# A second mixture whose matmul operands lie 32 bytes apart modulo 512 in SBUF instead of at equal remainders

## The chip, the core and the metric

The kernel runs on one core of a Trainium2 chip. The metric is the device time of one execution in microseconds (us), the median of several runs. The engines are called as the profile calls them: PE (TensorE matmuls), PEld (TensorE's weight loads, which overlap PE), DVE (VectorE), ACT (ScalarE), POOL (GpSimd) and SP (the queue that issues most DMAs).

## What is computed

Three layers follow each other, in fp32: a windowed attention over 4 batches, 8 heads, 576 positions, 64 dimensions; a first mixture, in which each of 2304 tokens goes to one of 8 experts; and a second one, dense, through which all 2304 tokens go. The change touches the last alone:

```python
def _moe_ref(x, ...):                       # first mixture, per expert e
    h = np.maximum(x[mask] @ w1[e], 0.0)    # 512 -> 1024
    out[mask] = gate_w[mask, None] * (h @ w2[e])

def _moe2_ref(x, w_in, w_out):              # second mixture
    h = x @ w_in                            # 2304x512 @ 512x2048
    g = h * np.cos(h)
    return (g @ w_out).astype(np.float32)   # 2304x2048 @ 2048x512
```

## The kernel before

**Three products for one.** Every large fp32 product is made of three matmuls on operands of type fp32r: each operand is split into a high part and a rest, and high x high, high x rest and rest x high are summed in PSUM. So `wi_a`, `yT`, `gg` and the others have a dimension of 2 (`a` or `b` in the code): part 0 and part 1.

**Roles.** In `nc.tensor.matmul(out, lhsT, rhs)` the second argument is loaded into the array as weights (128 columns of 4 bytes, 512 bytes in each partition), the third streams past it (the moving operand, 256 or 512 columns). The row of PEld for a matmul is the load of its weights; it runs while the matmul before it streams.

**Second mixture, up (`up2`, line 1325).** For a group of 4 times 128 tokens and a tile `f` of 128 hidden columns (16 of them) there are 12 matmuls: 4 pieces of the 512 inputs (`kk`) times 3 products. The weights are a slice of `wi_a` (f below 8) or `wi_b` (f from 8), the moving operand is `yT`, 512 columns:

```python
nc.tensor.matmul(ph, wi[:, a, fi, 128 * kk:128 * kk + 128], yT[:, b, kk], ...)
```

Behind it ACT and DVE form `r = ph * cos(ph)` and split it into `gg`.

**Second mixture, down (`down2`, line 1353).** Here `gg` is the weights and `wo_a` or `wo_b` the moving operand, 512 columns; again 12 matmuls for a tile `f` (4 token tiles times 3 products):

```python
nc.tensor.matmul(ACC[s][t], gg[:, a, cs], wo[:, b, fo], ...)
```

PE's order is 12 of up, 12 of down for the tile two steps before, 12 of up, and so on, over segments `segs` (line 1321). There are 5 groups of tokens; the last has 2 token tiles only, so that `yT` is 256 columns wide there, and its `gg` lies in the other `yT` tile (lines 1408 and 1409; the trace then calls it yT). Some `wi` and `wo` halves (the b ones) are converted from their 64-bit form while the mixture already runs (`conv`).

**First mixture (`up`, `down`).** The same three products, in blocks of 12, with a moving operand of 256 columns: weights `s1_*` and `s2_*` (trace: s), moving operands `xT*` and `hh`. Its last unit (`unit_parts`, line 1003) is turned round: weights `xT` and `hh2` (trace: hh), moving operand `s`, 512 columns.

**Where tiles lie.** Tiles are allocated in stacks from both ends of SBUF, so a tile's byte address in a partition follows from what was allocated before it. An unused tile (`gap0`, line 944, `gap3`, line 1310) shifts what comes behind it. All parts and slices of the tiles below are whole multiples of 512 bytes apart, so that one remainder modulo 512 holds for each tile. In the built program of the kernel before they are:

| place | weights (remainder) | moving operand (remainder) | weights minus moving |
|---|---|---|---|
| first mixture, up and down | s 320 | xT, hh 288 | +32 |
| first mixture, last unit | xT, hh2 288 | s 320 | -32 |
| second mixture, up | wi_a, wi_b 320 | yT 320 | 0 |
| second mixture, down | gg 320 (also in yT) | wo_a, wo_b 320 | 0 |

Of the kernel before, what the change touches and what calls it, by code (L numbers as in the profile page):

```python
# [8 lines left out]
F32 = mybir.dt.float32  # L9
# [20 lines left out]
def kernel(  # L30
# [42 lines left out]
    def pool(c, name, bufs, side="left"):  # L73
        return c.enter_context(tc.tile_pool(name=name, bufs=bufs, side=side, reuse_waits="tile"))
# [860 lines left out]
    wi_h = [wres.tile([128, 2, NA, KD * 128], F32R, name="wi_a")]  # L935
    wo_h = [wres.tile([128, 2, NA, DM], F32R, name="wo_a")]
    yt0 = pool(ctx, "yt0", 1)
    ytiles = [yt0.tile([128, 2, KD * 512], F32R, name="yT0")]
    W1, W2, HH, ACC = {}, {}, {}, {}
    NF = FF // 128  # L940
# [364 lines left out]

    with ExitStack() as c:
        wb = pool(c, "wb", 1, "right")
        wi_h.append(wb.tile([128, 2, NA, KD * 128], F32R, name="wi_b"))
        wo_h.append(wb.tile([128, 2, NA, DM], F32R, name="wo_b"))
        wb.tile([128, 32], F32, name="gap3")  # L1310
        hpi = wb.tile([128, 1], F32, name="hpi")
        fp = pool(c, "fp", 2, "right")
        yp = pool(c, "yp", 4, "right")
# [151 lines left out]
```

## Time and profile before

| | |
|---|---|
| median of 3 runs | 843.32 us (842.28 to 845.54) |
| the profiled execution, its own time | 844.73 us |
| its span, first to last instruction | 843.0 us |
| granted TensorE clock, mean | 0.989 of full speed |
| PE / DVE / ACT / POOL busy | 95% / 73% / 58% / 24% of the span |

Attention takes the first fifth of the span, the first mixture the time to 435 us, the second the rest. A row of the timeline merges instructions of one kind that follow each other: its time is from the first one's start to the last one's end. A matmul's own duration contains its latency, so that rows overlap; the time that a block costs is the distance between its start and the start of the next.

### The profile page before, as it was taken

How to read it: one execution, taken by the hardware profiler on the slowest of the kernel's cores; microseconds unless marked ns; L12 is line 12 of the kernel's file. 1: busy time of each engine (PE TensorE's matmuls, PEld its weight loads, DVE VectorE, ACT ScalarE, POOL GpSimd, SP SyncE). 2: the span in 40 equal slices, each digit the busy share in tenths (PEclk: the TensorE clock that was granted, in tenths of full speed). 3: DMA queues.
4: the chain of work that ended last, by engine and by line, in shares of the span. 5: the costliest groups of instructions: out<-in, count | busy, mean ns of one | idle time of the engine just before them, and what ended most of it. 6: DMA issues, size and time to landing. Idle time of an engine off the chain costs nothing. (4 is left out here: it accounts for less than half of the span.)

```text
span 843.0 us, 14736 instructions
## 1 busy us (share of the span) xinstructions
PE 801.4 (95%) x5269; PEld 705.8 (84%) x5269; DVE 614.7 (73%) x1463; ACT 492.1 (58%) x912; POOL 201.2 (24%) x259
## 2 busy tenths in 40 slices
PE   7899999979899999999999999999999999999996
PEld 5789888969799999999878778787788888888995
DVE  3866686668889999996749989896665555555562
ACT  6675677534557576664637676764554454444562
POOL 5655565510122132230001121112212001100100
PEclk9899999989999999999999999999999999999999
DMA  8555441044788888869433232501312001100000
GB/s 158 141 143 126 120 120 38 28 148 141 260 278 273 273 284 278 267 221 335 158 125 100 80 106 73 176 25 51 112 38 75 1 1 37 38 1 0 26 26 25
DMA packets 125134, 103.40 MB, mean 123 GB/s; under 512 B 61725, under 2 KB 105027, under 8 KB 125059
## 3 DMA queue, kind: packets, MB, share of 16 engines
q1 hardware_dynamic: 122099, 92.74, 36.3%
q0 software_dynamic: 2960, 9.70, 3.2%
q8 instruction: 42, 0.69, 0.3%
q14 instruction: 33, 0.27, 0.1%
HBM read 85.90 MB, written 16.52 MB: 121 GB/s over the span
## 5 line engine op out<-in xcount | busy, mean ns | idle before, releaser
L1079 PE MATMUL bk<-hh,s 128*128 128x256 f32 x864 | 117.7, 284 | 7.8 <-DVE y L1079 4.6
L1079 PEld LDWEIGHTS bk<-hh,s 128*128 128x128 f32 x864 | 107.8, 188 | 10.1 <-DVE y L1079 5.6
L1079 PE MATMUL bk<-xT,s 128*128 128x256 f32 x864 | 114.5, 282 | 1.7 <-DVE s L1079 1.1
L1079 POOL TENSOR_TENSOR lf<-lf,mag 128x512 f32<-128x512 f32 x32 | 46.9, 1467 | 282.1 <-DVE mag L1079 246.9
L1079 PEld LDWEIGHTS bk<-xT,s 128*128 128x128 f32 x864 | 107.4, 188 | 2.2 <-DVE s L1079 1.3
L1079 ACT CAST s<-r 128x1024 fp32r<-128x1024 f32 x72 | 75.2, 1050 | 54.4 <-DMA r<-in_moe_w_dram 40.4
L1079 PE MATMUL bk<-yT,wi_a 128*128 128x512 f32 (+1 forms) x480 | 104.4, 368 | 1.2 <-DVE yT L1079 0.8
L1079 PE MATMUL bk<-yT,wi_b 128*128 128x512 f32 (+1 forms) x480 | 105.0, 368 | 0.0
L1079 DVE TENSOR_TENSOR s<-r,s 128x1024 fp32r<-128x1024 f32 x72 | 94.3, 1313 | 13.6 <-ACT s L1079 13.2
L1079 ACT ACTIVATE r<-r 128x512 f32<-128x512 f32 (+1 forms) x80 | 47.2, 590 | 92.5 <-DVE r L1079 92.5
L1079 PEld LDWEIGHTS bk<-yT,wi_a 128*128 128x128 f32 x480 | 84.0, 188 | 17.3 <-DVE yT L1079 1.1
L1079 PEld LDWEIGHTS bk<-yT,wi_b 128*128 128x128 f32 x480 | 84.6, 188 | 15.7
L1079 DVE TENSOR_TENSOR r<-bk,r 128x512 f32<-128x512 f32 (+1 forms) x80 | 50.9, 636 | 62.1 <-ACT r L1079 61.4
L1079 PE MATMUL bk<-wo_b,gg 128*128 128x512 f32 x384 | 93.7, 391 | 2.5 <-DVE po L1079 1.1
L1079 PE MATMUL bk<-wo_a,gg 128*128 128x512 f32 x384 | 92.8, 390 | 0.6 <-DVE gg L1079 0.5
L1079 PEld LDWEIGHTS bk<-wo_b,gg 128*128 128x128 f32 x384 | 71.4, 188 | 19.7 <-ACT o L1079 1.5
L1079 PEld LDWEIGHTS bk<-wo_a,gg 128*128 128x128 f32 x384 | 71.8, 188 | 16.5 <-DVE gg L1079 1.5
L1079 DVE TENSOR_TENSOR gg<-r,gg 128x512 fp32r<-128x512 f32 x64 | 46.1, 720 | 34.3 <-ACT gg L1079 34.3
L494 PE MATMUL bk<-vt,pT 128*128 128x65 f32 x544 | 66.8, 276 | 0.1
L494 PEld LDWEIGHTS bk<-vt,pT 128*128 128x128 f32 x544 | 65.1, 195 | 1.2 <-issue 1.0
L1079 ACT CAST gg<-r 128x512 fp32r<-128x512 f32 x64 | 39.7, 620 | 41.1 <-DVE r L1079 40.2
L1079 DVE SCALAR_TENSOR_TENSOR r<-ki,bk 128x512 f32<-128x512 int32 (+1 forms) x80 | 50.4, 630 | 16.5 <-ACT ki L1079 15.9
(280 smaller groups left out, 1279.5 us busy)
## 6 DMA issues: line engine op xcount, KB each, us to landing
r<-in_moe_w_dram SPq DMA_DIRECT2D x72, 512.0 KB
y_dram<-y SPq DMA_DIRECT2D x19, 256.0 KB
rqk<-in_q_dram SPq DMA_DIRECT2D x32, 128.0 KB
rqk<-in_k_dram SPq DMA_DIRECT2D x32, 128.0 KB
vt<-in_v_dram SPq DMA_DIRECT2D x32, 128.0 KB
x_dram<-xt SPq DMA_DIRECT2D x16, 256.0 KB
f64x<-in_moe_w_in_dram SPq DMA_DIRECT2D x8, 512.0 KB
raw<-in_moe_w_dram SPq DMA_DIRECT2D x8, 512.0 KB
```

The lines of the kernel that those rows point to most:

```text
L494: self.last = op(*args, **kwargs)
L1079: r = op(*args, **kwargs)
```

## The change

Two unused tiles of 32 bytes are added, ahead of `yT0` and ahead of `wi_b`, and `gap3` shrinks from 128 to 64 bytes. No other line changes.

```diff
     yt0 = pool(ctx, "yt0", 1)
+    yt0.tile([128, 8], F32, name="gap1")
     ytiles = [yt0.tile([128, 2, KD * 512], F32R, name="yT0")]
...
         wb = pool(c, "wb", 1, "right")
+        wb.tile([128, 8], F32, name="gap2")
         wi_h.append(wb.tile([128, 2, NA, KD * 128], F32R, name="wi_b"))
         wo_h.append(wb.tile([128, 2, NA, DM], F32R, name="wo_b"))
-        wb.tile([128, 32], F32, name="gap3")
+        wb.tile([128, 16], F32, name="gap3")
         hpi = wb.tile([128, 1], F32, name="hpi")
```

In the built program `yT0`, `yT1`, `gg` and the work tiles of the second mixture (f64x, raw, mag, top, lf, ki, r, yg, gb, o, po) come to remainder 352, `wi_b` and `wo_b` to 384; `wi_a` and `wo_a` stay at 320, and nothing of the first mixture's operands moves:

| second mixture | weights | moving operand | weights minus moving | matmuls |
|---|---|---|---|---|
| up with wi_a | 320 | yT 352 | -32 | 384 of 512 columns, 96 of 256 |
| up with wi_b | 384 | yT 352 | +32 | 384 of 512 columns, 96 of 256 |
| down with wo_a | gg 352 | 320 | +32 | 432 of 512 columns |
| down with wo_b | gg 352 | 384 | -32 | 432 of 512 columns |

Each engine has the same instructions in the same order. One wait moves, on SP's queue, at the start of the second mixture, where the tiles of the second group of tokens are fetched (yg is a tile of tokens, gb its gates; names behind `waits` are the semaphores of engines and DMA queues). Before:

```order
L967 DMA yg<-y_dram 128x4x128 [waits DMAHW1_49,DMAHW2_49,DVE_49,DMAHW3_49,PE_49,Activation_49]
L968 DMA gb<-g_dram 128x128 [waits DMAHW4_49]
L967 DMA yg<-y_dram 128x4x128 [waits DMAHW5_49]
L968 DMA gb<-g_dram 128x128 [waits DVE_49,DMAHW6_49,PE_49,Activation_49]
L967 DMA yg<-y_dram 128x4x128 [waits DMAHW7_49]
```

And now:

```order
L968 DMA yg<-y_dram 128x4x128 [waits DMAHW1_49,DMAHW2_49,DVE_49,DMAHW3_49,PE_49,Activation_49]
L969 DMA gb<-g_dram 128x128 [waits DVE_49,DMAHW4_49,PE_49,Activation_49]
L968 DMA yg<-y_dram 128x4x128 [waits DMAHW5_49]
L969 DMA gb<-g_dram 128x128 [waits DMAHW6_49]
L968 DMA yg<-y_dram 128x4x128 [waits DMAHW7_49]
```

The wait for PE, DVE and ACT, which stood at the second gb, stands at the first, one yg and one gb earlier: the first gb tile, 32 bytes further on, now reaches into a tile of the first mixture that is released later.

## Rows read from the trace of the kernel before

**Rows 1.** Page, part 1: busy time, share of the span, instructions

```profile
PE 801.4 (95%) x5269; PEld 705.8 (84%) x5269; DVE 614.7 (73%) x1463; ACT 492.1 (58%) x912; POOL 201.2 (24%) x259
```

**Rows 2.** Windows: the second mixture in three stretches and as a whole

```profile
435.60:592.60 157.00, 153.10 (x662) 123.39 (x662) 133.79 (x220) 99.61 (x171) 28.59 (x21) 1.00 0.28 89
592.60:785.40 192.80, 192.76 (x851) 159.62 (x851) 110.47 (x162) 97.12 (x156) 20.88 (x17) 1.00 0.09 30
785.40:836.00 50.60, 50.60 (x313) 45.36 (x312) 27.81 (x69) 27.73 (x69) 4.96 (x5) 1.00 0.06 22
435.60:836.00 400.40, 396.45 (x1824) 328.38 (x1824) 272.07 (x449) 224.46 (x394) 54.42 (x43) 1.00 0.16 52
```

**Rows 3.** Chain that ended last, from 592 us: start, us, what

```profile
592.66 240.74 PE bk L1079 x1150
833.39 0.02 issue
833.42 0.70 DVE o L1079
834.12 0.27 issue
834.38 2.72 DMA out_dram<-o,tok_d
```

**Rows 4.** Waits of PE, 435 to 592 us: total us, times, longest

```profile
PE bk L1079 <- DVE po L1079: 1.1, 2, 0.9
PE bk L1079 <- ACT o L1079: 1.1, 1, 1.1
PE bk L1079 <- DVE yT L1079: 0.8, 1, 0.8
PE bk L1079 <- DVE gg L1079: 0.5, 1, 0.5
PE bk L1079 <- PEq L1281: 0.5, 1, 0.5
PE bk L1079 <- ACT gg L1079: 0.3, 1, 0.3
```

**Rows 5.** Timeline of PE, second mixture, 512 columns: start, us, what, count

```profile
603.22 2.88 PE L1079 MATMUL bk<-wo_b,gg 128*128 128x512 f32 x12
605.94 2.88 PE L1079 MATMUL bk<-yT,wi_b 128*128 128x512 f32 x12
```

**Rows 6.** Timeline of PE, second mixture's last group: 256 and 512 columns

```profile
793.82 7.36 PE L1079 MATMUL bk<-yT,wi_a 128*128 128x256 f32 x60
801.01 1.55 PE L1079 MATMUL bk<-wo_a,yT 128*128 128x512 f32 x6
802.40 1.60 PE L1079 MATMUL bk<-yT,wi_a 128*128 128x256 f32 x12
...
826.39 9.71 PE L1079 MATMUL bk<-wo_b,yT 128*128 128x512 f32 x42
```

**Rows 7.** Timeline of PE, first mixture, 256 columns

```profile
343.78 1.58 PE L1079 MATMUL bk<-xT,s 128*128 128x256 f32 x12
345.20 1.58 PE L1079 MATMUL bk<-hh,s 128*128 128x256 f32 x12
```

**Rows 8.** Timeline of PE, first mixture's last unit, 512 columns

```profile
425.37 1.56 PE L1079 MATMUL bk<-s,xT 128*128 128x512 f32 x6
426.77 1.55 PE L1079 MATMUL bk<-s,hh 128*128 128x512 f32 x6
```

**Rows 9.** Tile hh: durations min/median/max of the last unit's matmuls

```profile
L1079 PE MATMUL bk<-s,hh x24: 388/394/502, 426.8 to 433.4; 128*128 128x512 f32 x24
```

**Rows 10.** Timeline of PE, second mixture's start and a block behind a stall

```profile
435.68 11.16 PE L1079 MATMUL bk<-yT,wi_a 128*128 128x512 f32 x48 [0.46 <-PEq L1281]
446.68 5.60 PE L1079 MATMUL bk<-wo_a,gg 128*128 128x512 f32 x24
```

**Rows 11.** Tiles wi_a and wi_b on DVE: durations min/median/max

```profile
L1079 DVE TENSOR_TENSOR top<-top,wi_a x8: 676/680/1794, 244.4 to 309.4; 128x512 f32<-128x512 f32 x8
L1079 DVE TENSOR_TENSOR top<-top,wi_b x8: 676/678/693, 456.6 to 553.2; 128x512 f32<-128x512 f32 x8
```

**Rows 12.** Timeline of SP's queue and of DVE at the second group's fetch

```profile
440.32 0.40 SPq L967 DMA_DIRECT2D yg<-y_dram  x1
440.76 0.50 SPq L968 DMA_DIRECT2D gb<-g_dram  x1
441.31 0.42 SPq L967 DMA_DIRECT2D yg<-y_dram  x1
441.90 0.38 SPq L968 DMA_DIRECT2D gb<-g_dram  x1
...
452.14 1.78 DVE L1079 TENSOR_TENSOR yg<-yg,gb 128x512 f32<-128x512 f32 x1
```

## Prediction, made before the changed kernel ran

> **What bounds the kernel now.** I read the busy times first: PE is busy for 95% of the span, DVE for 73% [rows 1]. A busy PE may still be waiting, so I cut the second mixture into stretches [rows 2]. From 592.6 to 785.4 us PE is busy for 192.76 of 192.80 us, at the full granted clock; from 785.4 to 836 us for all of it. In the first stretch, 157 us long, it idles for about 4 us and DVE is busy for 133.79 us. The chain of waits agrees: its last long piece is 240.74 us of PE alone, 1150 matmuls, and behind it come only one eviction and one store [rows 3]. So in this half of the kernel the spacing of the matmuls is the time: 1824 matmuls in 400.4 us [rows 2].
>
> Then I read the spacing. At 512 columns 12 matmuls start 605.94 - 603.22 = 2.72 us apart, 226.7 ns each [rows 5]. At 256 columns 60 matmuls take 801.01 - 793.82 = 7.19 us, 119.8 ns each, and 120.0 without the first one, which is short [rows 6]. The difference, 106.7 ns for 256 columns, is one column per cycle of the 2.4 GHz level. What is left over is 13.3 ns per matmul, the same at both widths. Over 1824 matmuls that is 24.3 us, all that a better placing of the operands could bring if it removed the whole of it.
>
> **Does the placing matter at all?** The first mixture has weights and moving operand 32 bytes apart already, and there 12 matmuls of 256 columns take 345.20 - 343.78 = 1.42 us, 118.3 ns [rows 7], against 120.0 at equal remainders: 1.7 ns less. Its last unit has the distance the other way, at 512 columns. Six of its matmuls take 426.77 - 425.37 = 1.40 us, 233.3 ns [rows 8], and the six behind them, whose last lasts 394 ns by the median [rows 9], are (1.55 - 0.394) / 5 = 231.2 ns apart: together 232.3 ns, 5.7 ns more than at equal remainders. These two rows are the only ones on operands 32 bytes apart, and they point in opposite directions.
>
> The second of them needs care. At equal remainders too a block of 6 that stands behind 256-column matmuls takes 802.40 - 801.01 = 1.39 us, 231.7 ns [rows 6]. But there the excess dies out: the last 42, (9.71 - 0.39) / 41 = 227.3 ns on average [rows 6], are nearly at 226.7. The same behind a stall: the first 48 of the second mixture take 11.00 us, 229.2 ns each, and by the end of them the rate is the steady one [rows 10]. In the last unit the second six are no faster than the first to speak of. I read this as two modes: at equal remainders the stream settles after some ten matmuls into a regular spacing of 226.7 ns, and at 512 columns 32 bytes apart it stays at the rate of the unsettled ones, 232 to 233 ns.
>
> **The change, term by term.**
>
> 1. *512 columns, 1632 matmuls* (768 up, 864 down, by the diff's table). The price of +32 bytes at this width is in no row. The bounds: the first mixture's gain, -1.7 ns, from a row of another width but of this sign [rows 7], and the last unit's loss, +6.6 ns by its first six [rows 8], from a row of this width but, for half of the matmuls, of the other sign. I take +6.0, between the two blocks of six, for both signs, since the width is what the spacing hangs on and up and down alternate every 12 matmuls: a block that would settle has only 12 to do it in. 1632 x 6.0 = +9.8 us.
> 2. *What is already at that rate* does not get slower: 16 blocks of 6 behind 256 columns, 0.03 us each, and the matmuls behind the start and the stalls, about 0.12 us for the start [rows 10] and as an estimate half of that for each of eight stalls. About 0.9 us, so -0.9.
> 3. *256 columns, 192 matmuls*: -1.7 ns each as in the first mixture [rows 7], -0.3 us; at worst the few ns of term 1 with the other sign, under 1 us.
> 4. *Cover in the first stretch.* A slower PE gives DVE more time there. Of PE's waits those for gg and yT, 0.5 + 0.8 + 0.3 us, end with DVE's or ACT's work [rows 4] and shrink; those for an eviction (po, o), 2.2 us, come behind PE's own last matmul and stay. -0.8 us, between 0 and -1.6.
> 5. *DVE, ACT and DMA on the shifted tiles*: nothing. The same DVE operation takes 680 ns on work tiles at remainder 288 and 678 at 320 [rows 11].
> 6. *The moved wait on SP.* The first gb and the second yg behind it are issued when the second gb was, 441.90 instead of 440.76, so about 1.1 us later [rows 12]; DVE first reads them at 452.14. Those 10 us cover it; without the cover it would cost the 1.1 us once.
>
> Sum: 9.8 - 0.9 - 0.3 - 0.8 = +7.8 us. On the span of 843.0 us that makes 850.8, on the profiled execution's 844.73 us it makes 852.5, and on the median of the runs, 843.32 (1.4 below that execution), **851.1 us**, 0.9% slower.
>
> **The rivals.**
>
> *The sign decides.* Weights 32 bytes behind the moving operand gain as in the first mixture, 32 bytes ahead lose as in its last unit. By the diff's table the 512-column matmuls are then split evenly: 816 x 6.0 - 816 x 1.7 = 4.9 - 1.4 = +3.5, less about 0.8 for terms 2 and 4: 846.0 us. For it: both rows are then explained as they stand. Against it: the two blocks alternate, and a settled spacing hardly survives the change.
>
> *All gain as in the first mixture.* 1824 x 1.7 = 3.1 us less, 840.2 us. For it stands the one long and steady row [rows 7]; against it that it has the other width.
>
> *The left-over time goes.* If the 13.3 ns are a conflict of the weight load with the stream and 32 bytes resolve it at 512 columns, the kernel is faster. The point from which this decides is 2.6 ns per matmul (4.2 us over 1632); half of the 13.3 ns would bring 1632 x 6.7 = 10.9 us on a PE that has no cover over 243 us of it, and less in the first stretch, where DVE is busy for 85% [rows 2]: about 833 us. Against it: the first mixture, already 32 bytes apart, keeps 11.7 of its 13.3 ns [rows 7]. The Trainium skill, page "TensorE: Matmul & The Clock Gate", section "Back-to-back issue gap", gives N / 2.4 + 2.5 ns for an isolated matmul, 215.8 at 512 columns; this trace has 226.7, and if the change reached the page's figure it would bring some 17.8 us.
>
> *The placing does nothing.* The spacing does not hang on addresses, the 1.7 ns come from what else the first mixture does, and the last unit is slow because it never settles: 843.3 us. The trace speaks against it with two regular rates that differ where only address and surroundings do, 118.3 and 120.0 ns [rows 6, 7]. The Trainium skill says on the same page, in "Step-by-step: what each phase is for", that moving operand and weight load have a read port each, so that a load takes nothing from the running matmul; by that rule this rival is the right one, and the two rates do not fit it.
>
> **How the numbers follow.** A difference under 0.5%, 4.2 us, can hardly be told from none. The forecast, all 512-column matmuls unsettled, gets 0.48; its own range is 848 to 855, from term 1 at 4.5 to 6.6 ns with the other terms at their ends, up to 1 us for 256 columns and 1 us for SP. Sign decides: 0.20. No effect: 0.12. Gain as in the first mixture: 0.11. Left-over time goes: 0.09. Slower by over 0.5% (above 847.5): the 0.48 and 0.05 of the sign rival, 0.53. Faster (below 839.1): the 0.09 and 0.02 of the gain rival, 0.11. Within: 0.36. The range from 840.0 to 855.5 leaves out the last rival, a part of the gain rival and a worse loss at 256 columns, some 0.18.
>
> **What would show it.** Right: PE's timeline from 592 us on has blocks of 12 that start 2.78 to 2.80 us apart instead of 2.72, and PE's chain of 1150 matmuls is about 6 us longer; the stretch before 435 us is unchanged. The sign rival shows blocks of two lengths, wi_a and wo_b long, wi_b and wo_a short. The gain rivals show every block under 2.72 us. Wrong would also be a new wait of PE for yT near 474 us (the moved wait on SP), or blocks that still settle at 2.72.

## The result and the profile after

Four executions of the changed kernel took 851.92 to 855.1 us, median 852.37; four of the kernel before, run beside them, 842.28 to 845.54, median 843.87. The ratio is 1.0094, with a 95% interval from 1.007 to 1.0118: slower, by 8.5 us. A second comparison on one chip, with 10 executions against 31, gave medians of 851.59 and 846.61 us and a ratio of 1.0061 (1.0022 to 1.0100). So the loss is clear of no change, and its size is nearer to 5 us than the first comparison says; what is known of the difference comes below.

Page of the kernel after, part 1 (busy time, share of the span, instructions), beside [rows 1]:

```profile
span 850.5 us, 14736 instructions
PE 812.2 (96%) x5269; PEld 708.7 (83%) x5269; DVE 614.7 (72%) x1463; ACT 493.6 (58%) x912; POOL 200.2 (24%) x259
```

The same instructions, DVE as busy as before, PE busy for 10.8 us more. The timeline of PE of the kernel after, from the stretch in which PE waits for nothing, beside [rows 5]:

```profile
630.65 2.96 PE L1080 MATMUL bk<-yT,wi_a 128*128 128x512 f32 x12
633.45 2.96 PE L1080 MATMUL bk<-wo_a,gg 128*128 128x512 f32 x12
636.25 2.96 PE L1080 MATMUL bk<-yT,wi_a 128*128 128x512 f32 x12
639.05 2.96 PE L1080 MATMUL bk<-wo_a,gg 128*128 128x512 f32 x12
```

Every block of 12 now takes 2.80 us, 233.3 ns per matmul, where it took 2.72. In the first row the weights lie 32 bytes behind the moving operand (at the lower remainder: wi_a 320, yT 352), in the second 32 ahead (gg 352, wo_a 320): both cost the same. The windows of the second mixture, cut at the same matmuls as [rows 2] (the 1st, the 663rd, the first of the last group, the end), of the kernel after:

```profile
438.80:594.60 155.80, 155.27 (x662) 123.84 (x662) 133.94 (x220) 99.63 (x171) 28.64 (x21) 1.00 0.28 90
594.60:792.95 198.35, 198.35 (x851) 159.62 (x851) 110.58 (x161) 97.42 (x156) 20.83 (x17) 1.00 0.09 29
792.95:843.55 50.60, 50.60 (x313) 44.88 (x311) 27.93 (x69) 27.79 (x69) 5.01 (x5) 1.00 0.06 23
438.80:843.55 404.75, 404.22 (x1824) 328.35 (x1824) 272.45 (x449) 224.85 (x394) 54.47 (x43) 1.00 0.16 52
```

The second mixture is 4.35 us longer. The middle stretch is 5.55 us longer, 198.35 us against 192.80, the last one is as long as before, and the first, whose matmuls are slower too, is 1.2 us *shorter*: PE is busy there for 155.27 us instead of 153.10, and idle for 0.5 us instead of 3.9. What happened there stands in PE's waits, 438 to 595 us (total us, times, longest), of the kernel after, beside [rows 4]:

```profile
PE bk L1080 <- ACT xg L1080: 0.7, 1, 0.7
PE bk L1080 <- PEq L1282: 0.5, 1, 0.5
PE bk L1080 <- DVE yT L1080: 0.4, 1, 0.4
```

The first of these lies ahead of the second mixture. Gone are the waits for po, o and gg, 2.2 us for evictions among them; the one for yT is halved. The chain that ended last, beside [rows 3], shows where it does cost:

```profile
593.84 247.03 PE bk L1080 x1154
```

The piece of PE alone is 6.3 us longer, with four matmuls more in it, which are worth 0.9 us (an estimate, 4 x 0.233). Behind it come the same eviction and the same store.

The rest of this execution's difference lies ahead of the change: its second mixture starts at 438.80 us, 3.2 us later than before. Two windows of 10 us from the first mixture (PE busy, granted clock, DMA share, GB/s), kernel after first, kernel before second, and the first of the two from a control with all operands at the old remainders (`c1_moved_ident`, below) third:

```profile
250.00:260.00 10.00, 8.10 (x55) 0.85 0.92 280
400.00:410.00 10.00, 8.22 (x60) 0.86 0.58 205
```

```profile
250.00:260.00 10.00, 8.56 (x70) 1.00 0.96 299
400.00:410.00 10.00, 8.52 (x73) 1.00 0.43 141
```

```profile
250.00:260.00 10.00, 8.12 (x58) 0.88 0.91 288
```

In the kernel after the granted clock fell to its lower level, 1.2 GHz, for a while in each of the two, and 15 and 13 matmuls fewer stand there. At 0.118 us each [rows 7] that is 3.3 us, an estimate that agrees with the 3.2. In the first window no tile is in use that the change moves; in the second DVE fills yT0 and reads raw, which have moved. That the change is not needed for such a fall is shown by the control, and the changed kernel runs without one there in its second profile below. The executions of the second comparison agree: mean clocks from 0.970 to 0.989 and times from 841.34 to 854.22 us in 31 of the kernel before, clocks from 0.972 to 0.991 in 10 of the changed one.

### The profile page after: what moved, and what is told of

Its sections match the earlier page's. It is cut to its first block, busy times and chain, and to the rows that moved or that the text cites. A ratio compares the mean times of both kernels' runs of the same rounds, so it can differ in the third digit from the quotient of the medians.

```text
span 850.5 us, 14736 instructions
## 1 busy us (share of the span) xinstructions
PE 812.2 (96%) x5269; PEld 708.7 (83%) x5269; DVE 614.7 (72%) x1463; ACT 493.6 (58%) x912; POOL 200.2 (24%) x259
## 5 line engine op out<-in xcount | busy, mean ns | idle before, releaser
L1080 PE MATMUL bk<-hh,s 128*128 128x256 f32 x864 | 119.8, 287 | 7.4 <-DVE y L1080 3.6
L1080 PEld LDWEIGHTS bk<-hh,s 128*128 128x128 f32 x864 | 110.1, 192 | 9.6 <-DVE y L1080 4.4
L1080 PE MATMUL bk<-yT,wi_b 128*128 128x512 f32 (+1 forms) x480 | 107.4, 372 | 0.0
L1080 PE MATMUL bk<-yT,wi_a 128*128 128x512 f32 (+1 forms) x480 | 106.4, 372 | 0.9 <-PEq L1282 0.5
L1080 PE MATMUL bk<-wo_a,gg 128*128 128x512 f32 x384 | 94.7, 396 | 0.0
```

Of the source, the lines that this page charges most:

```text
L1080: r = op(*args, **kwargs)
```

## The experiments

The kernels below, the changed kernel itself and the two on the first mixture excepted, need more room in SBUF than is left. For them the identity tile, 512 bytes, moves from one pool to another, which keeps every remainder:

```diff
-    ident = const.tile([128, 128], F32, name="ident")
+    ident = rt.tile([128, 128], F32, name="ident")
```

Single executions are not compared by their time below, since what lies ahead of the second mixture scatters by over 10 us between them; the timelines are.

### Control: the identity tile moved, nothing else

> The identity tile (512 bytes) lies in another pool, so that 512 bytes are free for paddings later; all operands keep their remainders modulo 512. Every theory: no change, ratio within 0.5% of 1, blocks of 12 in the second mixture 2.72 us apart. If the changed kernel's 3.1 us ahead of the second mixture are chance dips of the clock, this kernel's runs have mean granted clocks that scatter like the changed kernel's (0.980 to 0.986); if the change causes them, this kernel stays at about 0.989.

Measured: ratio 0.9991 (0.9965 to 1.0017), blocks of 12 at 2.72 us. Its ten executions have mean clocks from 0.969 to 0.989, so dips of the clock come without the change. Its windows, cut as above:

```profile
437.20:592.70 155.50, 152.33 (x662) 123.61 (x662) 133.76 (x220) 99.80 (x171) 28.61 (x21) 1.00 0.28 90
592.70:785.50 192.80, 192.76 (x850) 159.59 (x851) 110.74 (x161) 96.92 (x156) 20.83 (x17) 1.00 0.10 30
```

The first stretch was 157.00 us in the kernel before and is 155.50 here with the same operands, so that 1.5 us there are scatter; the middle one is 192.80 again. In the first stretch PE is busy for 152.33 of 155.50 us, and DVE does the same 133.8 to 133.9 us of work in all three kernels.

### The changed kernel again

> The changed kernel once more. Placing theory: the second mixture, first up to last down, lasts 404 to 405 us against 400.0 before, blocks of 12 at 2.80 us, and what lies ahead of it starts it at 435.7 us plus 1.7 us for each chance dip of the clock, so that a run without more dips than before is 4 to 5 us slower (848) and not 8.5. Rival, that the change costs time ahead of the second mixture too: it starts at 438 us or later again, at mean clocks of 0.986 or less in every run, 852 us.

Measured: ratio 1.0061 (1.0022 to 1.0100). Its profiled execution had a mean clock of 0.991, started the second mixture at 433.8 us and took 847.58 us. Its windows:

```profile
433.80:590.00 156.20, 155.43 (x662) 123.78 (x662) 133.72 (x220) 99.72 (x171) 28.63 (x21) 1.00 0.28 89
590.00:788.40 198.40, 198.40 (x852) 159.68 (x852) 110.81 (x161) 97.61 (x156) 20.80 (x17) 1.00 0.09 29
```

So 198.4 us in the middle again, 405.15 for the whole, and no loss ahead of it. Against the kernel before (400.4) the change costs 4.4 and 4.75 us in two profiles, against the control (398.95) 5.8 and 6.2; that is the size of the second comparison's 5.0. Of the first comparison's 8.5 us, then, some 3 should lie ahead of the second mixture. In the one execution that was profiled they do, with the two falls of the clock; that it was so in the other three is likely by their mean clocks, 0.980 to 0.986, but not shown.

### Up alone 32 bytes apart

```diff
+    yt0.tile([128, 8], F32, name="gap1")
```

> Only yT moves (remainder 352, weights wi at 320); gg, wo and all else stay at equal remainders. Theory that each block settles by its own remainders: up blocks 2.80 us, down blocks back at 2.72 to 2.75 after some five matmuls, the second mixture about 2.5 us longer. Rival, that an unsettled block carries over into the next 12: up and down blocks both at 2.78 to 2.80, as long as the changed kernel's second mixture, 4.4 us longer.

In the last group gg lies in yT, so that down's weights are 32 bytes ahead there; the rows below lie ahead of it. Timeline of PE:

```profile
641.17 2.92 PE L1080 MATMUL bk<-wo_a,gg 128*128 128x512 f32 x12
643.93 2.97 PE L1080 MATMUL bk<-yT,wi_a 128*128 128x512 f32 x12
646.74 2.92 PE L1080 MATMUL bk<-wo_a,gg 128*128 128x512 f32 x12
649.49 2.73 PE L1080 MATMUL bk<-yT,wi_a 128*128 128x512 f32 x11
```

Up blocks take 2.81 us, down blocks 2.75 to 2.76. The means of a down block's twelve spacings, over the 33 blocks from 605 us to the last group, are 240.9, 224.1, 230.9, 236.0, 228.1, 232.9, 231.0, 226.1, 226.9, 227.0, 226.1, 226.9 ns: unsettled for seven matmuls, then at the settled rate. So settling goes by a block's own remainders, and a neighbour 32 bytes apart costs a block at equal ones 0.036 us. The rival of a carry-over through the whole block falls. So does another one, that the shifted tiles of ACT and DVE (ki, r, gg, o, po) slow PE: here they lie as in the kernel before, and up has 2.81 us all the same. The times do not fit as well. In the profile the second mixture takes 404.1 us between the starts of its first and last matmul against 400.0: 4.1 us more, where about 2.5 were expected. The timed ratio, 0.9992 (0.9965 to 1.0020), allows a loss of 1.7 us at most by its interval. The blocks are what this run shows; why the executions are no longer is open.

### One sign: weights behind the moving operand

```diff
+    yt0.tile([128, 8], F32, name="gap1")
+        wb.tile([128, 8], F32, name="gap2")
```

> yT at 352 with wi at 320, gg at 288 with wo at 320: the weights lie 32 bytes behind the moving operand in up and in down, one sign alone. Theory that any 32 bytes unsettle the stream at 512 columns: all blocks 2.80 us, second mixture 404 to 405 us as with the change. Rival, that the alternation of the two signs keeps the changed kernel unsettled: with one sign the stream settles, at 2.72 us or below.

```profile
640.60 2.96 PE L1080 MATMUL bk<-wo_a,gg 128*128 128x512 f32 x12
643.40 2.96 PE L1080 MATMUL bk<-yT,wi_a 128*128 128x512 f32 x12
646.20 2.96 PE L1080 MATMUL bk<-wo_a,gg 128*128 128x512 f32 x12
```

All blocks of 12 ahead of the last group (where gg lies in yT, 32 bytes ahead) take 2.80 us, and the ratio is 1.0069 (1.0036 to 1.0102), as with the change. It is not the alternation of signs that keeps the stream from settling.

### Other distances

The same two paddings, with 64, 128, 256 and 96 bytes each, and once 160 ahead of `yT0` and 192 ahead of `wi_b`.

> yT and gg placed so that the weights lie 64 bytes behind the moving operand in up and in down. Theory that only equal remainders let the stream settle: blocks of 12 at 2.80 us as with 32 bytes. Rival, that the distance itself sets a conflict: another spacing, below 2.72 us if 64 bytes clear what 32 do not.

> The same with 128 bytes, a quarter of the 512 that a weight tile takes. Theory that only equal remainders settle: 2.80 us. Rival, that the distance sets a conflict: another spacing than 32 and 64 bytes give. If the remainder that counts is not the one modulo 512 but modulo 128, the stream settles at 2.72 us.

> The same with 256 bytes, half of the 512. Theory that only equal remainders modulo 512 settle: 2.80 us. If the remainder modulo 256 counts: 2.72 us. Rival, that the largest distance clears a conflict: below 2.72 us.

> Weights 160 bytes behind the moving operand in up, 192 in down. So far 32 and 128 bytes give 2.80 and 2.79 us per block, 64 gives 2.76, and 256 gives 2.72 like 0, so that the remainder modulo 256 seems to count. If it does, 160 and 192 are 96 and 64 bytes ahead: theory that no distance goes below the settled rate: both blocks between 2.72 and 2.80 us, 192 like 64 at about 2.76. Rival, that a distance not yet tried clears the left-over time: one of the two blocks below 2.72 us.

> Weights 96 bytes behind the moving operand in up and in down. Theory that no distance goes below the settled rate: blocks between 2.72 and 2.80 us. Rival, that an untried distance clears the left-over time: below 2.72 us.

A block of each, by the timeline of PE: 64 bytes (first fence), 128, 256, then 160 and 192 together (160 in up), and 96:

```profile
641.36 2.93 PE L1080 MATMUL bk<-yT,wi_a 128*128 128x512 f32 x12
644.13 2.92 PE L1080 MATMUL bk<-wo_a,gg 128*128 128x512 f32 x12
```

```profile
641.91 2.96 PE L1080 MATMUL bk<-wo_a,gg 128*128 128x512 f32 x12
644.71 2.96 PE L1080 MATMUL bk<-yT,wi_a 128*128 128x512 f32 x12
```

```profile
642.41 2.88 PE L1080 MATMUL bk<-yT,wi_a 128*128 128x512 f32 x12
645.13 2.88 PE L1080 MATMUL bk<-wo_a,gg 128*128 128x512 f32 x12
```

```profile
643.65 2.96 PE L1080 MATMUL bk<-yT,wi_a 128*128 128x512 f32 x12
646.45 2.96 PE L1080 MATMUL bk<-wo_a,gg 128*128 128x512 f32 x12
```

```profile
643.44 2.96 PE L1080 MATMUL bk<-yT,wi_a 128*128 128x512 f32 x12
646.24 2.96 PE L1080 MATMUL bk<-wo_a,gg 128*128 128x512 f32 x12
```

| weights behind the moving operand by | 0 | 32 | 64 | 96 | 128 | 160 (up) | 192 (down) | 256 |
|---|---|---|---|---|---|---|---|---|
| us per block of 12, 512 columns | 2.72 | 2.80 | 2.75 to 2.77 | 2.79 to 2.80 | 2.79 to 2.80 | 2.80 | 2.79 to 2.80 | 2.72 |

256 bytes settle as 0 does, 128 do not: that fits a remainder modulo 256. The last group's 60 matmuls of 256 columns agree; at 256 bytes they take 7.19 us, as at 0 [rows 6]. 64 bytes were a surprise, about half way; 192, which modulo 256 is 64 the other way, did not share it, against what I had written. The run with 64 bytes has 64 the other way as well: in its last group gg lies in yT, 64 bytes ahead of wo_b, and the last 42 matmuls, beside [rows 6], are

```profile
825.61 9.96 PE L1080 MATMUL bk<-wo_b,yT 128*128 128x512 f32 x42
```

or (9.96 - 0.39) / 41 = 233.4 ns, without settling. So at 64 bytes the sign counts, 230 ns behind and 233 ahead, and 192 behind does as 64 ahead. No distance goes below 2.72 us: the 13.3 ns that are left over at equal remainders are not cleared by any of the seven tried. Distances that are no multiple of 32 bytes were not tried.

A rival is that not the distance counts but the remainder of each tile by itself. At 256 columns the runs speak against it: weights 32 ahead give 118.3 ns with 320 and 288 [rows 7], and much the same with 384 and 352 (up with wi_b in the last group of the changed kernel, 1.41 to 1.42 us per block); weights 32 behind give 116.7 ns with 256 and 288 (below) and 116.8 with 320 and 352. At 512 columns equal remainders were run at 320 alone (and 64 with 320), so that the stream settles at any equal pair is not shown.

### The first mixture: the other sign, and equal remainders

Its 256 columns are the other width. In one kernel the weights lie 32 bytes behind (hh's pool goes ahead of the weights' pool, and 32 bytes are put ahead of `xTs`), in the other gap0 is taken out, so that hh has its weights' remainder and xT has not:

```diff
+    rt.tile([128, 8], F32, name="gap4")
     xTs = [rt.tile([128, 2, KD, SLOTS], F32R, name=f"xT{j}") for j in range(2)]
...
+    hp_ = pool(bc, "hp", 2, "right")
     wp = pool(bc, "wp", 1, "right")
-    wp.tile([128, 8], F32, name="gap0")
     s1s = ...
     s2s = ...
+    wp.tile([128, 8], F32, name="gap0")
-    hp_ = pool(hc, "hp", 2, "right")
```

```diff
     wp = pool(bc, "wp", 1, "right")
-    wp.tile([128, 8], F32, name="gap0")
```

> The second mixture as before; in the first mixture the weights s lie 32 bytes behind the moving operands xT and hh (remainder 256 against 288) instead of 32 ahead. The changed kernel's last group had 256 columns with this sign at 116.8 ns each, with the other at 118.0, where the first mixture has 118.3. Theory that sign and width set the spacing: blocks of 12 of 256 columns at 1.40 us instead of 1.42, over 144 blocks 2.6 us where PE sets the pace, and less where weights arrive late: 0 to 2.6 us faster. Rival, that the last group's rate comes from its surroundings: 1.42 us, no change.

> The second mixture as before; in the first, the padding gap0 is taken out, so that hh comes to remainder 320, equal to its weights s, while xT stays at 288. Theory that equal remainders settle at 32 cycles over the width: down blocks (hh) of 256 columns at 1.44 us instead of 1.42, up blocks (xT) still at 1.42. Rival, that the price of a distance has nothing to do with the width: down blocks faster than 1.42 us, as equal remainders are at 512 columns.

Timelines of PE, weights behind first, then hh at equal remainders:

```profile
343.32 1.56 PE L1079 MATMUL bk<-hh,s 128*128 128x256 f32 x12
344.72 1.56 PE L1079 MATMUL bk<-xT,s 128*128 128x256 f32 x12
346.12 1.56 PE L1079 MATMUL bk<-hh,s 128*128 128x256 f32 x12
```

```profile
341.68 1.58 PE L1078 MATMUL bk<-xT,s 128*128 128x256 f32 x12
343.09 1.60 PE L1078 MATMUL bk<-hh,s 128*128 128x256 f32 x12
344.53 1.58 PE L1078 MATMUL bk<-xT,s 128*128 128x256 f32 x12
```

Weights behind: 1.40 us per block, 116.7 ns, against 1.42 [rows 7]. Equal: the hh block takes 1.44 us, 120.0 ns, and its xT neighbours 1.41 to 1.42. So at 256 columns the order is turned round: equal remainders are the slowest, and the sign counts. The gain of 0.02 us per block did not reach the total: 1.0015 (0.9978 to 1.0052) over 12 executions; over 144 blocks it would be 2.9 us if PE set the pace in all of them, and the interval allows 1.9 us at most. No version was found that beats the kernel before.

### The same blocks in two places

Only `yT1` moves by 32 bytes, which puts the up blocks of the second and of the fourth group of tokens apart, and with them the last group's down blocks, whose gg lies in yT1:

```diff
+    yt1.tile([128, 8], F32, name="gap1")
     ytiles.append(yt1.tile([128, 2, KD * 512], F32R, name="yT1"))
```

> Only yT1 moves by 32 bytes, so that the up blocks of the second and the fourth group of tokens are 32 bytes apart (16 blocks each) and all others equal, as before. The second group's blocks lie among the first 662 matmuls of the second mixture, where the change made no difference to the time (156.98 us before, 155.80 with the change), the fourth group's lie behind, where PE waits for nothing. By the run with up alone apart an up block costs 0.083 us more and the down block behind it 0.036. Theory that the first stretch is bound by DVE and ACT and absorbs a slower PE: the first 662 matmuls take 155 to 157 us, and the 1162 behind them 243.06 + 16 x 0.119 = 245.0 us, or a little less. Rival, that the first stretch is as long by chance: it is 1.9 us longer as well, about 158.9 us.

Windows: the first 662 matmuls, and the 384 of the fourth group with those that overlap its ends; then the same two of the kernel before:

```profile
449.95:605.60 155.65, 153.57 (x662) 123.68 (x662) 133.85 (x220) 99.55 (x171) 28.64 (x21) 1.00 0.29 90
717.30:804.90 87.60, 87.60 (x386) 71.24 (x385) 46.66 (x68) 42.52 (x69) 7.36 (x6) 1.00 0.06 19
```

```profile
435.65:592.65 157.00, 153.11 (x662) 123.39 (x662) 133.79 (x220) 99.66 (x171) 28.59 (x21) 1.00 0.28 89
703.85:789.65 85.80, 85.80 (x386) 71.27 (x385) 46.71 (x68) 42.47 (x69) 7.34 (x6) 1.00 0.06 19
```

The fourth group became 1.8 us longer, where 16 x 0.119 = 1.9 were expected. Of the second group's 16 blocks 13 lie in the first stretch, and they cost nothing that stands out of its scatter (155.65 us, the control's 155.50): PE is busy for 1.2 us more than in the control and waits for 1.1 us less. The rival, with 13 x 0.119 = 1.5 us more, would be at 157.0 by the control and at 158.5 by the kernel before. One profile is little against a scatter of 1.5 us, but the others agree: from the first to the 663rd start it is 155.5 to 157.0 us in the five profiles whose second mixture stands at 0 or 256 bytes, 155.5 to 156.2 in eight of the nine others, and 157.8 in the one at 128 bytes. The matmuls behind the first 662 came to 245.5 us, 2.4 more than before and half a microsecond over what was expected: I had left out three up blocks of the second group, which still lie there (0.36 us), and the last group (0.2 us).

## Why the prediction was right, and where it was not

**Right: the sign and the mechanism on PE.** The forecast stood on two modes, settled at equal remainders and unsettled at 32 bytes apart, at 512 columns with either sign. The blocks came out at 2.80 us, the upper end of the 2.78 to 2.80 written down, for both signs and in every place; the run with up alone apart shows the settling inside a block, matmul by matmul.

**Term 1, the size.** I took 6.0 ns, between the blocks of six at 231.2 and 233.3. Measured: 233.3 - 226.7 = 6.6 to 6.7 ns, the first six's value [rows 8]; 10% too small. The 231.2 was a misreading: I took the last matmul of that block at the median of 394 ns, but it has the minimum of [rows 9], 388, and the five spacings are then (1.55 - 0.388) / 5 = 232.4 ns.

**Terms 2 and 3, the last group.** Of the kernel after:

```profile
801.37 7.17 PE L1080 MATMUL bk<-yT,wi_a 128*128 128x256 f32 x60
808.38 1.56 PE L1080 MATMUL bk<-wo_a,yT 128*128 128x512 f32 x6
833.70 9.95 PE L1080 MATMUL bk<-wo_b,yT 128*128 128x512 f32 x42
```

The 60 matmuls with wi_a took 808.38 - 801.37 = 7.01 us, 116.8 ns against 119.8, so 3 ns less and not 1.7; all 192 of 256 columns gave back 0.4 us, not 0.3. Of blocks of six there are 9, not the 16 that term 2 counts; they are at 1.40 us against 1.39. The 42 behind them, one piece, had settled before and became 0.24 us slower [rows 6]. Gains and losses cancel: the last stretch is unchanged at 50.6 us.

**Term 4, the cover, is the step that failed.** "Of PE's waits those for gg and yT ... shrink; those for an eviction (po, o), 2.2 us, come behind PE's own last matmul and stay. -0.8 us". In fact the whole first stretch absorbed the slower PE: its 662 matmuls made PE busy for 2.2 us more (2.9 against the control), and its waits shrank by 3.4 (2.6), those for evictions among them. The rows show why. PE's last block before an eviction and ACT's first copies of that eviction, kernel before and then after:

```profile
528.16 2.88 PE L1079 MATMUL bk<-wo_a,gg 128*128 128x512 f32 x12
534.21 1.06 ACT L1079 COPY o<-bk 128x512 f32<-128x512 f32 x2
```

```profile
531.97 2.96 PE L1080 MATMUL bk<-wo_a,gg 128*128 128x512 f32 x12
537.10 1.54 ACT L1080 COPY o<-bk 128x512 f32<-128x512 f32 x3
```

Before, ACT came to its copies 3.2 us after PE's block had ended at 531.04, with the change 2.2 us after; it does other work first. DVE's first po comes 2.8 us behind PE's block before and 1.6 us with the change. So the evictions hung not on PE's last matmul but on engines that reached them late, and with a slower PE they were less late. That the engine that evicts has a queue of its own in front of the eviction is what I left out. With the measured terms the sum is about 970 x 6.65 = 6.5 us for the 512-column matmuls behind the first stretch, less 0.4 for those of the last group that were unsettled already, and less 0.4 for the 192 of 256 columns: 5.7, where the two profiles have 248.95 against 243.40 us, 5.55.

**The total agrees partly by chance.** +7.8 us were forecast and +8.5 measured at first, but the second mixture gave 4.4 to 4.8 and the larger comparison 5.0. The prediction's term 4 was about 3 us too small, and the first comparison held some 3 us more than the second mixture explains; the two happen to be alike. One of the signs written down, an unchanged stretch before 435 us, did not come true in that first profile, whose second mixture starts 3.2 us late, and did in the second, which has no such delay (433.80 us).

**Terms 5 and 6** cost nothing: DVE's busy time is 614.7 us in both, and SP's queue has the first gb at 443.65 us and DVE's first read of it at 455.38, 11.7 us later:

```profile
443.09 0.40 SPq L968 DMA_DIRECT2D yg<-y_dram  x1
443.65 0.38 SPq L969 DMA_DIRECT2D gb<-g_dram  x1
```

The 1.1 us that the moved wait was to hold back the first gb did not appear either: it is issued 4.85 us after the second mixture's start, where it was 5.16 [rows 12].

**The rivals.** That the sign decides fell with both blocks at 2.80 us, and with one sign alone at the same rate. (Its first sentence has the words the wrong way round: by the table of remainders the first mixture's weights are 32 bytes ahead, its last unit's behind. The signs of wi_a to wo_b go by the table, and the price is the same, as the matmuls are split evenly.) That all gain as in the first mixture fell too: its gain belongs to 256 columns, and is measured against a settled rate that has the same 13.3 ns left over at either width, while 32 bytes apart 10.0 to 11.7 ns are left over at 256 columns and 20.0 at 512. The left-over time went at no distance. That the placing does nothing fell with every timeline at 32 bytes. The Trainium skill ("TensorE: Matmul & The Clock Gate", "Step-by-step: what each phase is for") states that a weight load takes no SBUF read bandwidth from the running matmul. By that alone the spacing would not hang on where the two operands lie; for these fp32r operands it does, by 6.6 ns per matmul at 512 columns. Whether the load takes reads after all, or something else does it, the runs do not show.

**Still open** is what settles. The runs show that it goes by the distance between the two operands, as far as the pairs tried can tell, that 0 and 256 bytes are alike, that it takes some five to fifteen matmuls (five behind 256 columns, seven behind a block 32 bytes apart, fifteen behind a stall), and that what is left over then is 13.3 ns, 32 cycles at 2.4 GHz, at either width; they don't show what in the chip does it.

## What to carry to other kernels

Read the spacing of a matmul stream from the starts of its blocks and compare it with columns over the clock, for each width apart: a rule on operand addresses that gained at one width lost at another, and one block in the trace of the right width was worth more than a long steady row of the wrong one. A slower or faster PE is worth its price only in the stretches in which it waits for nothing; for the others look at what the engines behind the waits do, evictions included, before calling a wait fixed. Where single executions scatter by more than the effect, compare the stretch that changed and not the total.

## What the hardware showed that I had not expected

At 512 columns the spacing of fp32r matmuls depends on the distance between weights and moving operand: 226.7 ns at 0 and 256 bytes, about 230 with the weights 64 behind, 233 with them 64 ahead, 32 either way, and 96, 128, 160 or 192 behind. At 256 columns the order is the reverse: 120.0 ns at 0, 118.3 with the weights 32 bytes ahead, 116.7 with them 32 bytes behind. And on one chip the same kernel's executions went from 841.34 to 854.22 us, with dips of the granted clock to the lower level at places that change from run to run.
